# Scratch for the sums of x in a tile of its own, the keys turned behind the queries' scan, and one more tile of lag for the second layer

## The chip, the cores and the metric

The kernel runs on one core of one Trainium2 chip (trn2). The metric is the device time of one execution in microseconds (us); the median of three runs is given. A core has five engines that run their own queues in order and wait for one another by semaphores: TensorE (PE, with its weight loads PEld), VectorE (DVE), ScalarE (ACT), GpSimd (POOL) and SyncE (SP, which here only issues transfers). Transfers (DMA) run on 16 DMA engines.

## The reference

Two parts follow one another. The first is a gated linear attention over 4 batches, 8 heads, 768 positions and a head size of 48; the second a two-layer network with a squared relu, on 3072 tokens with a model size of 384 and a hidden size of 2048.

```python
f = 1 / (1 + exp(-f_logit))
for t in range(768):                       # per batch and head
    state = f[t][:, None] * state + outer(k[t], v[t])
    y[t] = q[t] @ state
x = y of all heads side by side            # 3072 x 384
h = maximum(x @ w_in, 0)
out = (h * h) @ w_out
```

## The kernel before

**Blocks, units, tiles.** The 768 positions are cut into 6 blocks of 128 positions (512 tokens with the 4 batches). The attention of a block is done in 4 units of two heads each; 16 of them (those of blocks 2 to 5, called 2_0 to 5_3 here) run inside the stream of the second part. The second part of a block has 16 tiles f of 128 hidden rows. A tile has a first layer (`up`, nine matmuls of 512 columns: three slices of the model size, each as three products of float16 halves), a squared relu with a split into halves gh and gl, and a second layer (`down`, nine matmuls: for each third e of the output the products of w's upper half with gl, w's lower half with gh, upper half with gh). The order of blocks is 1, second half of 0, 2, 3, 4, 5; tiles are counted through from the start of this order, so that block 2 has tiles 24 to 39 and blocks 3, 4, 5 have 40 to 55, 56 to 71, 72 to 87.

**The second layer lags.** In blocks 2 to 5 (`flow`) `owe` puts the three second-layer pieces of a finished tile into a queue, and `take` issues pieces from its front. In block 2, each tile takes three pieces and adds three; in a tile listed in `SKIP` it takes none, and the queue stays three longer from then on. gh and gl have `GBUF` = 5 buffers each.

**Pairs.** In blocks 3 to 5 the first layer of two tiles is done together (`pair`): eleven narrow steps of three matmuls with 256 columns, in place of six steps with 512. It needs sums of quarters of w (made earlier) and of x: t1 to t4 of `make_sums_x`. These are ten POOL subtractions and additions in float32 (line 586) into a scratch, which ACT (line 589) and DVE (line 590) then split into halves. They are issued at the last four tiles of the block before. The scratch lies in a hole of the tiles of w_out of f = 8 to 11: a w tile has 768 float32 columns as two halves of 384; the float16 weights take the first 192 float32 columns of each half, and `work` takes 128 columns behind them in either half. The results t1 to t4 go to holes of the tiles 0 to 7. A pair's relu, square and split run on ACT and POOL (`later`, lines 510 to 517) after the next pair's first two products.

**Units in the stream.** Each unit has a slot, a tile number of `SLOTS`: 12, 14, 19, 21 for block 2, 22, 27, 29, 33 for block 3, 35, 39, 43, 47 for block 4, 51, 55, 59, 63 for block 5. In the slot, TensorE computes the outputs of the unit before (stage Y), the added state and the scores of this one (D, lines 888, and S, line 907); D reads kn, the keys turned by 32x32 squares. The stages before it are hung on earlier tiles by `STAGE_AT` (blocks up to 2) and `STAGE_AT_LATER` (blocks 3 to 5): (tiles from the slot, place in the tile, stages). L loads f, k and q into fkq. G makes the gates (ACT, line 760), K scans the gates backwards for the keys' factors (line 767), k multiplies the keys (780), Q scans forwards for the queries' factors (789), q multiplies the queries (797). t (`squares`) turns the keys within squares on DVE (line 846) and writes them to DRAM in four transfers (`steps`, line 852); b (`back`) loads them in their new order as kn (line 859; one buffer). K, Q and t use the same row of fkq (`rr`) for their results. The fourth unit of a block has no keys of its own (its rows are gathered from the other three by stages m and l). SP issues transfers in the order of the program, and each waits for what it reads. Stage b stands three tiles before the slot; where the unit before has its slot in between, it stands in that unit's slot. Transfers x<-ys (lines 1026), which complete a block's x, are issued in the slot after the fourth unit's.

**The scratch called junk.** Line 205 (`sizes`, ACT) writes absolute values of weights that nobody reads, one pass per tile from tile 28 on, 32 in all; only their sum counts. It takes 384 of the 1560 float32 columns of a tile with one buffer.

Of the kernel before, what the change touches and what calls it, by code (L numbers as in the profile page):

```python
# [12 lines left out]
F32 = mybir.dt.float32  # L13
# [10 lines left out]
P = 128  # L24
B, H, S, D = 4, 8, 768, 48
DM, DFF = 384, 2048
# [5 lines left out]
NT = B * TB  # L32
NZ = B * NC
CZ = C + 1
ROWS = 64 + D
NJ = DM // P
# [36 lines left out]

STAGE_AT = ((-8, 1, "L"), (-6, 1, "GK"), (-5, 0, "v"), (-5, 1, "Q"), (-4, 1, "t"))
STAGE_AT_LATER = (
    (-8, 1, "L"), (-6, 1, "G"), (-5, 0, "vK"), (-5, 0.7, "k"), (-5, 1, "t"), (-3, 0, "Q"), (-3, 0.7, "q"),
)
LAST_AT = ((-5, 0, "v"),)

SLOTS = (12, 14, 19, 21, 22, 27, 29, 33, 35, 39, 43, 47, 51, 55, 59, 63, 67)  # L80
# [2 lines left out]
NQ = NT // 2  # L83
HB, HA = slice(0, NQ), slice(NQ, NT)
PAIRED = 3
SKIP = 6, 10
T_HOLES, T_WORK, S_WORK = (0, 4), 8, 12
S_FROM, S_STEPS = 10, 6

LATE = ((0, 2), (0.5, 2)), ((0.7, 2), (1, 2))  # L90
# [23 lines left out]
class Moe:  # L114
# [86 lines left out]
    def sizes(self, f, i):  # L201

        if not (f or i):
            self.junk = self.third_of("junk")[0][:, :DM]
        self.nc.scalar.activation(
            self.junk, self.w[f, i][:, 0], AF.Abs, scale=1.0 if i else 4.0,
            accum_out=self.sums[:, 2 * f + i : 2 * f + i + 1],
        )
# [324 lines left out]

    def work(self, f):

        return self.full[f, 1].bitcast(F32)[:, :, DM // 2 : DM // 2 + P]

    def make_sums_w(self, q):

        G = self.nc.gpsimd  # L540
        add, sub = ALU.add, ALU.subtract
        f, f2 = 2 * q, 2 * q + 1
        (a11, a12), (a21, a22) = (
            [[self.w[k, 0][:, i, j * P : (j + 1) * P] for i in range(2)] for j in range(2)] for k in (f, f2)
        )
        s, u = (self.work(S_WORK + 2 * (q % 2) + i)[:, 0] for i in range(2))
        out = self.sums_w(q)

        def split(n, t):
            G.tensor_copy(out=out[n][:, 0], in_=t)  # L550
            yield
            G.tensor_tensor(out=out[n][:, 1], in0=t, in1=out[n][:, 0], op=sub)
            yield

        def chain(t, *terms):
            for o, i0, i1, op in terms:
                G.tensor_tensor(out=o, in0=i0, in1=i1, op=op)  # L557
                yield

        yield from chain(s, (s, a21[0], a22[0], add), (s, s, a21[1], add), (s, s, a22[1], add))  # L560
        yield from split(0, s)
        yield from chain(u, (u, a11[0], a21[0], sub), (u, u, a11[1], add), (u, u, a21[1], sub))
        yield from split(2, u)
        yield from chain(s, (s, s, a11[0], sub), (s, s, a11[1], sub))
        yield from split(1, s)
        yield from chain(s, (s, a12[0], s, sub), (s, s, a12[1], add))
        yield from split(3, s)

    def make_sums_x(self, blk, x):

        nc, G = self.nc, self.nc.gpsimd
        add, sub = ALU.add, ALU.subtract
        wide = lambda t: t.rearrange("p (a n) -> p a n", a=2)
        (b11, b12), (b21, b22) = (
            [[wide(x[j][:, i, h]) for i in range(2)] for h in (HA, HB)] for j in range(2)
        )
        t1, t2, t3, t4 = (self.work(T_WORK + i) for i in range(4))
        out = self.sums_x(blk)
        for terms in (
            ((t1, b12[0], b11[0], sub), (t1, t1, b12[1], add), (t1, t1, b11[1], sub)),  # L580
            ((t3, b22[0], b12[0], sub), (t3, t3, b22[1], add), (t3, t3, b12[1], sub)),
            ((t2, t3, b11[0], add), (t2, t2, b11[1], add)),
            ((t4, b21[0], t2, sub), (t4, t4, b21[1], add)),
        ):
            for o, i0, i1, op in terms:
                G.tensor_tensor(out=o, in0=i0, in1=i1, op=op)  # L586
            yield
        for n, t in ((0, t1), (2, t3), (1, t2), (3, t4)):
            nc.scalar.copy(out=wide(out[n][:, 0]), in_=t)
            nc.vector.tensor_tensor(out=wide(out[n][:, 1]), in0=t, in1=wide(out[n][:, 0]), op=sub)  # L590
            yield

    def third_of(self, name):
# [72 lines left out]
def fast_path(ctx, tc, moe, ident, low, fkqT, vN, w, w4, out):  # L666
    nc = tc.nc
    V, G = nc.vector, nc.gpsimd
# [24 lines left out]
        out=mask0, in_=mask0, compare_op=ALU.is_ge, fill=0.0, base=0, pattern=[[1, TB]], channel_multiplier=-1,  # L693
    )
    G.memset(mask, 1.0)
    for r in (0, C):
        G.affine_select(
            out=mask[r : r + C], in_=mask[r : r + C], compare_op=ALU.is_ge, fill=0.0,
# [441 lines left out]
    with tc.manual_schedule(engines={ET.PE, ET.SP, ET.DVE, ET.Activation, ET.Pool}):  # L1140
# [6 lines left out]
        part = []  # L1147
# [5 lines left out]
        def hook(k, n, at, do):  # L1153
            while n >= len(order[k][1]):
                k, n = k + 1, n - len(order[k][1])
            hooks[k].setdefault((max(n, 0), at), []).append(do)
# [28 lines left out]
        back = 0  # L1185
        for un, last, at, soon, then in zip((*later, None), (None, *later), SLOTS, (*later[1:], None, None), (*SLOTS[1:], None)):
            if un:
                for n, place, stage in (STAGE_AT if un.early else STAGE_AT_LATER) if un.own else LAST_AT:
                    hook(0, at + n, place, lambda un=un, stage=stage: un.stage(stage))
                if un.own:  # L1190

                    if at - 3 > back:
                        hook(0, at - 3, 1, lambda un=un: un.stage("b"))
                    back = at

            def slot(un=un, last=last, soon=soon if soon and soon.own and then - 3 <= at else None):
                for who, stage in (last, "Y"), (un, "DS"), (last, "HX"), (un, "rMC"), (soon, "b"), (un, "ml" * bool(un and un.own)):
                    if who:
                        who.stage(stage)
                if last and not last.own:  # L1200
                    last.stage("hg")

            hook(0, at, 0.7, slot)
            if un:
                hook(0, at + 1, 0, lambda un=un: un.stage("s"))
# [34 lines left out]
        for blk in range(PAIRED, NBLK):  # L1240
            n = 2 * NF + LO + (blk - PAIRED) * NF - 4
            for at, place in ((0, 1), (1, 0.5), (1, 1), (2, 0.5), (2, 1), (3, 0), (3, 0.5), (3, 1)):
                hook(0, n + at, place, lambda blk=blk: advance_sums(blk, lambda: moe.make_sums_x(blk, xs[blk]), 1))
        for k, (blk, fs) in enumerate(order):
# [5 lines left out]
            if blk > 1:  # L1250
# [3 lines left out]
                if blk == NBLK - 1:  # L1254
                    obs = moe.third_of("ob_last")
                    items[-1:] = [(f,) for f in fs[-2:]]
                moe.flow(hooks[k], items, SKIP if blk == 2 else (), owed if blk == 2 else None)
            else:
# [157 lines left out]
@with_exitstack  # L1416
def tile_kernel(ctx: ExitStack, tc: tile.TileContext, fkqT, vN, w, w4, out):
    nc = tc.nc
    const = ctx.enter_context(tc.tile_pool(name="const", bufs=1))
    ident = const.tile([P, P], F32, name="ident")  # L1420
    low = const.tile([P, NBLK * NJ, B * NC], F32, name="low")
    sums = const.tile([P, (2 + NBLK) * NF + NBLK * NJ], F32, name="sums")
    moe = Moe(ctx, tc, const, sums, out)
    moe.hidden(ctx)
    with ExitStack() as fast:
        rv, obs = fast_path(fast, tc, moe, ident, low, fkqT, vN, w, w4, out)


    with tc.If(rv > 0):
        with ExitStack() as gen:  # L1430
            general_path(gen, tc, moe, ident, fkqT, vN, w, out)
        for e in range(NJ):
            nc.sync.dma_start(obs[e], out[NBLK - 1, e * P : (e + 1) * P])

    for e in range(NJ):
        for n, cs in tails(e):

            (nc.sync if n else nc.scalar).dma_start(out[NBLK - 1, e * P : (e + 1) * P, cs], obs[e][:, cs])
# [61 lines left out]
```

## Time and profile before

| | |
|---|---|
| median of 3 runs | 509.65 us (509.09 to 511.13) |
| profiled execution | 510.53 us, span 508.8 us |
| TensorE busy | 457.5 us (90%), mean granted clock 0.973 |
| ACT, DVE, POOL busy | 306.5, 280.0, 209.8 us |
| DMA | 47.90 MB, mean 94 GB/s |

The span runs from the first to the last instruction of the profiled execution. The granted clock is the share of TensorE's full clock (2.4 GHz) that it was given; the lower level is half of it. An engine's wait is the idle time ahead of an instruction, put down to what ended it.

### The profile page before, as it was taken

The page shows a single profiled execution, that of the slowest core. Times are in us where ns is not written, and L with a number is a line of the kernel's source. Part 1 is how long each engine was busy: PE and PEld are TensorE (multiplying, and loading weights), DVE is VectorE, ACT ScalarE, POOL GpSimd, SP SyncE. Part 2 cuts the span into 40 slices and gives each one's busy share as a digit, 9 for nine tenths or more (in the row PEclk, how much of TensorE's full clock was granted, in tenths as well). Part 3 has the DMA queues.
Part 4 walks back from the last instruction along what each step waited for, and adds up shares of the span by engine and source line. Part 5 has one row for each costly group of instructions (what it writes and reads, how often), then busy time and mean ns, then how long its engine had stood idle before and what let it go on. Part 6 is the DMA issues. An engine that isn't in the chain of part 4 may idle for free.

```text
span 508.8 us, 12206 instructions
## 1 busy us (share of the span) xinstructions
PE 457.5 (90%) x4903; PEld 262.0 (51%) x4906; DVE 280.0 (55%) x512; ACT 306.5 (60%) x709; POOL 209.8 (41%) x337
## 2 busy tenths in 40 slices
PE   8999899999998989998799899769999868999995
PEld 4655544444554535544266466436656534565652
DVE  8999826895646666656275455536524212324222
ACT  4679839855485546867358856537856532573650
POOL 5456436994865456440401321632131271313220
PEclk9999999999999999999799999889999987999998
DMA  8977075517354445143334041403200000100002
GB/s 301 279 279 236 14 252 196 205 36 160 82 147 114 99 122 135 22 130 54 96 71 138 20 119 25 125 10 63 79 1 2 12 6 0 63 0 1 1 0 70
DMA packets 65296, 47.90 MB, mean 94 GB/s; under 512 B 47440, under 2 KB 50768, under 8 KB 65232
## 3 DMA queue, kind: packets, MB, share of 16 engines
q1 hardware_dynamic: 64640, 46.19, 32.1%
q0 software_dynamic: 448, 0.73, 0.6%
q8 instruction: 40, 0.66, 0.5%
q14 instruction: 24, 0.20, 0.1%
q10 hardware_dynamic: 144, 0.13, 0.1%
HBM read 35.61 MB, written 7.86 MB: 85 GB/s over the span
## 4 chain that ended last, share of the span: by engine, by line
PE 37%; issue 16%; ACT 13%; POOL 11%; DVE 11%; DMA 8%; SPq 3%; POOLq 0%; DVEq 0%; ACTq 0%
PE po L365 16%; PE ph L309 10%; POOL gl L517 4%; PE cross L460 3%; POOL w L586 3%; ACT gh L514 3%; DMA raw<-in_w_dram 3%; DMA fkq<-in_fkqT_dram 3%; ACT st L510 2%; DMA steps<-fkq 2%; POOL w L192 2%; DVE gl L352 2%; PE line L460 2%; PE ds L907 1%; DVE fkq L789 1%
## 5 line engine op out<-in xcount | busy, mean ns | idle before, releaser
L365 PE MATMUL po<-gh,w 128*128 128x512 f16 x570 | 174.4, 388 | 18.3 <-POOL w L586 18.3
L365 PEld LDWEIGHTS <-w 128*128 128x128 f16 x864 | 84.0, 99 | 119.0 <-POOL w L586 20.4
L517 POOL TENSOR_TENSOR gl<-st,gh 128x512 f16<-128x512 f32 x46 | 54.0, 1195 | 173.4 <-ACT gh L514 173.4
L365 PE MATMUL po<-gl,w 128*128 128x512 f16 x288 | 111.2, 386 | 12.6 <-POOL gl L517 11.0
L309 PE MATMUL ph<-x,w 128*128 128x512 f16 x441 | 103.3, 380 | 3.2 <-DVE x L1019 2.5
L460 PEld LDWEIGHTS <-w 128*128 128x128 f16 x759 | 75.9, 100 | 35.2 <-issue 9.3
L505 ACT ACTIVATE st<-st 128x512 f32<-128x512 f32 x46 | 29.0, 631 | 86.5 <-DVE st L500 85.9
L309 PEld LDWEIGHTS <-w 128*128 128x128 f16 (+1 forms) x459 | 44.5, 98 | 57.4 <-issue 3.8
L352 DVE TENSOR_TENSOR gl<-ph,gh 128x512 f16<-128x512 f32 x48 | 32.8, 683 | 56.9 <-ACT gh L331 56.9
L327 ACT ACTIVATE ph<-ph 128x512 f32<-128x512 f32 x49 | 28.7, 586 | 54.1 <-PE ph L309 54.1
L500 DVE TENSOR_TENSOR st<-cross,st 128x512 f32<-128x512 f32 x23 | 15.9, 692 | 47.9 <-PE cross L460 47.9
L460 PE MATMUL cross<-x,w 128*128 128x256 f16 x276 | 38.4, 276 | 1.1 <-DVE ys L1019 0.9
L557 POOL TENSOR_TENSOR w<-w,w 128x128 f32<-128x128 f32 (+1 forms) x72 | 36.5, 507 | 4.3
L460 PE MATMUL cross<-w,w 128*128 128x256 f16 x207 | 35.3, 281 | 2.8 <-DVE st L489 1.6
L789 DVE TENSOR_TENSOR_SCAN fkq<-fz,dz 128x520 f32<-128x520 f32 x18 | 23.2, 1289 | 18.7 <-DMA steps<-fkq 18.3
L460 PE MATMUL line<-x,w 128*128 128x256 f16 x207 | 31.3, 280 | 0.0
L192 POOL TENSOR_TENSOR w<-wa,w 128x384 f16<-128x384 f32 x29 | 30.1, 1042 | 2.0
L187 POOL CAST w<-wa 128x384 f16<-128x384 f32 x29 | 19.9, 687 | 26.7 <-DVE wa L176 22.9
L767 DVE TENSOR_TENSOR_SCAN fkq<-fz,dr 128x520 f32<-128x520 f32 x18 | 23.3, 1295 | 12.2 <-ACT fz L760 12.2
L331 ACT ACTIVATE gh<-ph 128x512 f16<-128x512 f32 x48 | 28.7, 598 | 1.6
L328 ACT ACTIVATE ph<-ph 128x512 f32<-128x512 f32 x49 | 28.5, 582 | 1.5
L489 DVE COPY st<-cross 128x256 f32<-128x256 f32 x23 | 9.7, 420 | 35.7 <-PE cross L460 35.5
(184 smaller groups left out, 803.2 us busy)
## 6 DMA issues: line engine op xcount, KB each, us to landing
raw<-in_w_dram SPq DMA_DIRECT2D x33, 383.8 KB, 6.0
fkq<-in_fkqT_dram SPq DMA_DIRECT2D x15, 768.0 KB, 5.2
vn<-in_vN_dram SPq DMA_DIRECT2D x24, 192.0 KB, 4.9
steps<-fkq SPq DMA_DIRECT2D x48, 64.0 KB, 2.2
out_dram<-ob SPq DMA_DIRECT2D x12, 256.0 KB, 2.1
kn<-steps SPq DMA_DIRECT2D x13, 224.0 KB, 3.5
fkq<-in_fkqT_dram SPq DMA_DIRECT2D x9, 256.0 KB, 4.9
last_kq<-fkq SPq DMA_DIRECT2D x28, 64.5 KB, 3.1
```

The source lines that it names most:

```text
L192: (eng or nc.vector).tensor_tensor(out=w[:, 1], in0=a, in1=high, op=ALU.subtract)
L309: self.nc.tensor.matmul(self.ph[f], lhsT=w[:, i], rhs=x[:, j], start=first and n == 0, stop=last and n == 2)
L327: nc.scalar.activation(ph, ph, AF.Relu, scale=R_SCALE if self.half else 1.0)
L328: nc.scalar.activation(ph, ph, AF.Square)
L331: nc.scalar.activation(gh, ph, AF.Copy, accum_out=self.sums[:, n : n + 1])
L352: self.nc.vector.tensor_tensor(out=gl, in0=self.ph.pop(f), in1=gh if self.half else gh.bitcast(F32), op=ALU.subtract)
L365: self.nc.tensor.matmul(po[e], lhsT=l, rhs=r, start=f == fs[0] and i == 0, stop=f == fs[-1] and i == 2,)
L460: self.nc.tensor.matmul(out, lhsT=w[:, i], rhs=x[:, j], start=first and n == 0, stop=True, skip_group_check=True)
L505: nc.scalar.activation(st[:, r], st[:, r], AF.Relu, scale=R_SCALE)
L517: nc.gpsimd.tensor_tensor(out=wide(gl), in0=st[:, i::2], in1=wide(gh), op=ALU.subtract)
L557: G.tensor_tensor(out=o, in0=i0, in1=i1, op=op)
L789: V.tensor_tensor_scan(out=pp, data0=self.fz[:, : NZ * CZ], data1=dz, initial=0.0, op0=ALU.mult, op1=ALU.add)
```

## The change

1. The scratch for the sums of x moves from the holes of w tiles into the tile of which line 205 uses the first 384 columns: four contiguous pieces of 256 columns from column 512 on. The scratch for the sums of w stays where it was.
2. For units of blocks 3 to 5, Q moves from (-3, 0) to (-5, 1), q from (-3, 0.7) to (-3, 0), t from (-5, 1) to (-3, 0.7). Stage b moves from (-3, 1) to (-2, 0) (`BACK`); where the rule for "in between" holds for both places, b is issued in both.
3. `SKIP` gets tile 1 of block 2 besides 6 and 10, so that the second layer lags four tiles from block 2's tile 10 on, where it lagged three.

```diff
@@ -73,8 +73,9 @@
 
 STAGE_AT = ((-8, 1, "L"), (-6, 1, "GK"), (-5, 0, "v"), (-5, 1, "Q"), (-4, 1, "t"))
 STAGE_AT_LATER = (
-    (-8, 1, "L"), (-6, 1, "G"), (-5, 0, "vK"), (-5, 0.7, "k"), (-5, 1, "t"), (-3, 0, "Q"), (-3, 0.7, "q"),
+    (-8, 1, "L"), (-6, 1, "G"), (-5, 0, "vK"), (-5, 0.7, "k"), (-5, 1, "Q"), (-3, 0, "q"), (-3, 0.7, "t"),
 )
+BACK = -2, 0
 LAST_AT = ((-5, 0, "v"),)
 
 SLOTS = (12, 14, 19, 21, 22, 27, 29, 33, 35, 39, 43, 47, 51, 55, 59, 63, 67)
@@ -83,8 +84,8 @@
 NQ = NT // 2
 HB, HA = slice(0, NQ), slice(NQ, NT)
 PAIRED = 3
-SKIP = 6, 10
-T_HOLES, T_WORK, S_WORK = (0, 4), 8, 12
+SKIP = 1, 6, 10
+T_HOLES, S_WORK = (0, 4), 12
 S_FROM, S_STEPS = 10, 6
 
 LATE = ((0, 2), (0.5, 2)), ((0.7, 2), (1, 2))
@@ -201,7 +202,9 @@
     def sizes(self, f, i):
 
         if not (f or i):
-            self.junk = self.third_of("junk")[0][:, :DM]
+            junk = self.gp.tile([P, NJ * NZ * CZ], F32, tag="part", name="junk", bufs=1)
+            self.junk = junk[:, :DM]
+            self.work_x = [junk[:, NT + i * NQ : NT + (i + 1) * NQ] for i in range(4)]
         self.nc.scalar.activation(
             self.junk, self.w[f, i][:, 0], AF.Abs, scale=1.0 if i else 4.0,
             accum_out=self.sums[:, 2 * f + i : 2 * f + i + 1],
@@ -533,7 +536,7 @@
 
     def work(self, f):
 
-        return self.full[f, 1].bitcast(F32)[:, :, DM // 2 : DM // 2 + P]
+        return self.full[f, 1].bitcast(F32)[:, 0, DM // 2 : DM // 2 + P]
 
     def make_sums_w(self, q):
 
@@ -543,7 +546,7 @@
         (a11, a12), (a21, a22) = (
             [[self.w[k, 0][:, i, j * P : (j + 1) * P] for i in range(2)] for j in range(2)] for k in (f, f2)
         )
-        s, u = (self.work(S_WORK + 2 * (q % 2) + i)[:, 0] for i in range(2))
+        s, u = (self.work(S_WORK + 2 * (q % 2) + i) for i in range(2))
         out = self.sums_w(q)
 
         def split(n, t):
@@ -570,11 +573,10 @@
 
         nc, G = self.nc, self.nc.gpsimd
         add, sub = ALU.add, ALU.subtract
-        wide = lambda t: t.rearrange("p (a n) -> p a n", a=2)
         (b11, b12), (b21, b22) = (
-            [[wide(x[j][:, i, h]) for i in range(2)] for h in (HA, HB)] for j in range(2)
+            [[x[j][:, i, h] for i in range(2)] for h in (HA, HB)] for j in range(2)
         )
-        t1, t2, t3, t4 = (self.work(T_WORK + i) for i in range(4))
+        t1, t2, t3, t4 = self.work_x
         out = self.sums_x(blk)
         for terms in (
             ((t1, b12[0], b11[0], sub), (t1, t1, b12[1], add), (t1, t1, b11[1], sub)),
@@ -586,8 +588,8 @@
                 G.tensor_tensor(out=o, in0=i0, in1=i1, op=op)
             yield
         for n, t in ((0, t1), (2, t3), (1, t2), (3, t4)):
-            nc.scalar.copy(out=wide(out[n][:, 0]), in_=t)
-            nc.vector.tensor_tensor(out=wide(out[n][:, 1]), in0=t, in1=wide(out[n][:, 0]), op=sub)
+            nc.scalar.copy(out=out[n][:, 0], in_=t)
+            nc.vector.tensor_tensor(out=out[n][:, 1], in0=t, in1=out[n][:, 0], op=sub)
             yield
 
     def third_of(self, name):
@@ -1189,11 +1191,12 @@
                     hook(0, at + n, place, lambda un=un, stage=stage: un.stage(stage))
                 if un.own:
 
-                    if at - 3 > back:
-                        hook(0, at - 3, 1, lambda un=un: un.stage("b"))
+                    n, place = (-3, 1) if un.early else BACK
+                    if at + n > back:
+                        hook(0, at + n, place, lambda un=un: un.stage("b"))
                     back = at
 
-            def slot(un=un, last=last, soon=soon if soon and soon.own and then - 3 <= at else None):
+            def slot(un=un, last=last, soon=soon if soon and soon.own and then + (-3 if soon.early else BACK[0]) <= at else None):
                 for who, stage in (last, "Y"), (un, "DS"), (last, "HX"), (un, "rMC"), (soon, "b"), (un, "ml" * bool(un and un.own)):
                     if who:
                         who.stage(stage)
```

## Rows read from the trace of the kernel before

**Rows 1.** The page, busy time of each engine, share of the span, instructions
```profile
PE 457.5 (90%) x4903; PEld 262.0 (51%) x4906; DVE 280.0 (55%) x512; ACT 306.5 (60%) x709; POOL 209.8 (41%) x337
```

**Rows 2.** TensorE's waits: us in total, times, longest
```profile
PE po L365 <- POOL w L586: 18.3, 5, 5.4
PE po L365 <- POOL gl L517: 11.0, 19, 0.8
PE ph L309 <- DVE x L1019: 2.5, 1, 2.5
PE ph L971 <- DVE gl L352: 2.1, 3, 1.2
...
PE po L365 <- DVE part L642: 1.4, 1, 1.4
```

**Rows 3.** Timeline of TensorE, 237 to 252 us: start, us, line, tiles, [idle before]
```profile
237.56 2.11 PE L309 MATMUL ph<-x,w 128*128 128x512 f16 x9
239.51 0.38 PE L365 MATMUL po<-gl,w 128*128 128x512 f16 x1
245.33 1.03 PE L365 MATMUL po<-gh,w 128*128 128x512 f16 x2 [5.44 <-POOL w L586]
...
248.71 2.48 PE L309 MATMUL ph<-x,w 128*128 128x512 f16 x9
```

**Rows 4.** Windows behind the five stalls; PEclk is the third number from the end
```profile
245.30:252.00 6.70, 6.67 (x22) 2.68 (x23) 1.63 (x2) 1.88 (x5) 2.88 (x5) 0.69 0.16 47
328.30:334.00 5.70, 4.59 (x21) 2.64 (x21) 2.63 (x4) 4.39 (x11) 2.25 (x3) 0.73 0.23 70
337.40:343.00 5.60, 5.56 (x25) 2.94 (x26) 2.06 (x4) 0.00 (x0) 0.00 (x0) 0.70 0.07 12
413.10:419.00 5.90, 4.78 (x21) 2.73 (x21) 0.42 (x1) 3.48 (x8) 2.60 (x4) 0.71 0.00 0
421.40:428.00 6.60, 6.56 (x25) 3.19 (x26) 1.09 (x3) 0.00 (x0) 0.00 (x0) 0.58 0.00 0
```

**Rows 5.** Instructions of line 586: ns least/median/most, first and last start
```profile
L586 POOL TENSOR_TENSOR w<-w,x x21: 667/669/672, 241.7 to 420.7; 128x256 f32<-128x256 f32 x21
```

**Rows 6.** DVE's waits, as above
```profile
DVE fkq L789 <- DMA steps<-fkq: 18.3, 5, 5.1
```

**Rows 7.** Timeline of DVE, 142 to 158.5 us
```profile
146.50 1.13 DVE L846 STREAM_TRANSPOSE fkq<-fkq 128x512 f32<-128x512 f32 x1
...
153.40 1.25 DVE L789 TENSOR_TENSOR_SCAN fkq<-fz,dz 128x520 f32<-128x520 f32 x1 [5.08 <-DMA steps<-fkq]
154.57 0.66 DVE L352 TENSOR_TENSOR gl<-ph,gh 128x512 f16<-128x512 f32 x1
...
158.02 0.68 DVE L797 TENSOR_TENSOR fkq<-fkq 128x512 f32<-128x512 f32 x1
```

**Rows 8.** The page's groups: busy, mean ns of one | idle before
```profile
L331 ACT ACTIVATE gh<-ph 128x512 f16<-128x512 f32 x48 | 28.7, 598 | 1.6
```

**Rows 9.** Line 852, the transfers of steps, from issue to landing
```profile
DMA to landing us min/median/max: 2.1/2.2/3.8
```

**Rows 10.** Line 859, the load of kn, from issue to landing
```profile
DMA to landing us min/median/max: 3.2/3.5/5.1
```

**Rows 11.** Timeline of SP, 209 to 240 us (issues, waits between them included)
```profile
214.10 2.86 SPq L852 DMA_DIRECT2D steps<-fkq  x4
...
218.64 4.70 SPq L859 DMA_DIRECT2D kn<-steps  x2
```

**Rows 12.** Timeline of SP, 316 to 335 us
```profile
318.53 5.17 SPq L1026 DMA_DIRECT2D x<-ys  x6
323.80 0.61 SPq L750 DMA_DIRECT2D fkq<-in_fkqT_dram  x1
```

**Rows 13.** Timeline of ACT, 324 to 338 us
```profile
325.47 1.28 ACT L505 ACTIVATE st<-st 128x512 f32<-128x512 f32 x2 [2.49 <-DVE st L500]
329.02 0.63 ACT L760 ACTIVATE fz<-fkq 128x512 f32<-128x512 f32 x1 [2.27 <-DMA fkq<-in_fkqT_dram]
```

## The prediction

> **What bounds the kernel now.** I read the page first: TensorE is busy 457.5 of 508.8 us, every other engine at most 60% [rows 1]. So I asked what TensorE waits for. Two names hold two thirds of the waiting: POOL's line 586 with 18.3 us in 5 waits, and POOL's line 517 with 11.0 us in 19 [rows 2]. Below them stand waits on DVE (lines 1019, 352, 642), 6.0 us together.
>
> Line 586 makes the sums of x. The timeline of TensorE shows how it gets in the way [rows 3]. A step of the second layer issues three matmuls per e: upper half of w with gl, lower half of w with gh, upper half with gh. At 239.51 the first runs; the next stands for 5.44 us until POOL is done. The upper half is free, the lower is not. The scratch of before is two pieces of the same w tile (columns 192 to 319 of either half, in float32): from the first piece to the end of the second, that range covers the lower half of the weights. I conclude that TensorE waits for a range, not for data: it never reads those sums here. After the stall nine matmuls that took 2.11 us at 237.56 take 2.48 at 248.71: the granted clock has fallen to 1.2 GHz for a while. In the stretches behind the five stalls it is 0.58 to 0.73 on average [rows 4].
>
> Line 517 (gl of a pair) is the end of a chain, copy, square, gh, gl, that starts with the next pair; the second layer wants it 4 us later, and each pair loses up to 0.8 us [rows 2].
>
> On DVE the queries' scan of line 789 waits 18.3 us in 5 waits for the transfers of `steps` [rows 6]: the keys' turn and the scan use the same row of fkq, and the turn is written first. At 146.50 the turn, at 153.40 the scan, 5.08 us idle [rows 7]; behind it in the queue stood line 1019, for which TensorE then waited 2.5 us [rows 2].
>
> **The change part by part.** Terms are taken against the profiled run, 510.5 us (its span is 508.8).
>
> *Scratch of its own.* The 30 POOL instructions stay and keep 128x256 elements; all forms took 0.67 us [rows 5], and I cost the contiguous form the same. What goes is the overlap: 18.3 us [rows 2]. With the stalls goes the slow clock behind them: one minus the granted clock, times the stretch, is 2.1 + 1.5 + 1.7 + 1.7 + 2.8 = 9.8 us [rows 4]. Bounds for this: 5 (new stalls keep the clock low) to 9.8. Scratch is bufs=1 in a tile that ACT's line 205 writes in columns 0 to 383, the sums in 512 to 1535; rows 3 show that disjoint ranges don't wait.
>
> *SKIP at tile 1.* One more tile of second-layer work (three entries, nine matmuls) stays in the queue. A pair takes six entries; before, three old ones stood ahead of the new, now six, so a pair's gl is first read at the start of the pair after next, about 5 us later than now. The largest wait was 0.8, so all 11.0 us go. gh and gl have five buffers; four tiles in flight fit. At tile 1 itself TensorE skips the wait for line 642 (1.4 us). But two first-layer steps come back to back, and the tile after needs a bank that DVE frees behind three 0.7 us pieces of line 642 and the turn: I put 0.9 us there (0 to 2).
>
> *Queries before the turn.* The scan no longer waits. On TensorE that is worth 2.5 + 1.4 + 1.5 = 5.4 us (of the 2.1 us on line 352, 0.6 come from two back-to-back first-layer steps of the older skips, and stay) [rows 2]. Bounds: 0, if DVE is late again, to 6.
>
> What it costs: the turn, the four `steps` transfers and the load of kn now start 3 tiles before the slot in which TensorE reads kn (stage D); what queues behind a late kn is everything on TensorE. From the end of that tile's first layer: three ACT passes of 0.60 [rows 8], line 352 with 0.66, the turn 1.13 [rows 7], four issues of which the last comes some 2.0 after the first [rows 11], landing 2.2 (up to 3.8) after that [rows 9], kn 3.5 (3.2 to 5.1) [rows 10]. That is 11.3 us, 14.5 with the slowest landings. For the way TensorE needs three tiles of twice 1.95 us (nine matmuls, 237.56 to 239.51), 11.7 us [rows 3], and about 1 more, an estimate, for the outputs of the unit before: 12.7. In a plain unit kn is just in time. Not plain are: unit 3_0 (slot 22), whose turn stands behind slot 19's DVE pieces (155.2 to 158.0, 2.8 us) [rows 7], and which is now loaded twice: it is queued at tile 20 by the new rule and again in slot 21, and the second load of the one kn buffer waits for the first. How that looks is seen for unit 4_0, loaded twice already: two issues stretch over 4.70 us, and the second starts when the first has landed [rows 11]. So 11.3 + 2.8 + 3.5 = 17.6 against 14.7 (a slot lies between, some 2 us): 2.9 us. Unit 4_0 (slot 35): 14.8 against 12.7: 2.1. Unit 3_1 (slot 27), with one step of 1.95 skipped on the way: 0.3. The paired units have two thirds of a pair and a whole one, 18 wide matmuls and 33 half as wide a pair, 0.217 us for a wide one, 12.4 us, and the outputs: 0. I add 0.7 for transfers in each other's way: 6 us, between 0 and 14 (slowest landings at the five unpaired units).
>
> A page of the Trainium skill speaks against this part: DMA: Bandwidth & Descriptors, Rules for kernel authors, says to issue a transfer early and wait for it late, so that its fixed cost is covered. The change issues one later. No row shows the loads uncovered yet; by that rule the second rival below would be the forecast.
>
> *What stands behind the stalls.* With line 586 out of the way, ACT comes next in block 3's last pairs: its gates of 329.02 waited 2.27 us for a load of fkq [rows 13], issued at 323.80 behind six transfers that last 5.17 us [rows 12]. Nothing in the change moves those. Today TensorE stands still there anyway. Then it will begin the pair near 326, while ACT is in the passes of 325.47 [rows 13], do 12 narrow and three wide matmuls (1.95 us), and wait from about 327.9 for ACT's copy of its first products, which can end at 330.8 (329.65, then line 205 and the copy, 0.6 each): 3.0 us (0 to 4.5, with the clock). Block 2's like wait goes, since the turn's transfers no longer stand in SP's queue before it.
>
> Sum: 510.5 - 18.3 - 9.8 - 11.0 - 5.4 + 6.0 + 3.0 + 0.9 = 475.9. The median of the runs, 509.65, is 0.9 below the profiled run, and a fall of the clock behind a new stall would cost about as much: 476 us. All the gains without new waits give 466; the bounds together 460 to 495.
>
> **Rivals.**
> 1. *The turned keys come late everywhere.* For: plain units have only 1.4 us to spare, and one load took 5.1. Against: medians. If each of the nine units loses 3 us, 27 instead of 6: 497 us. The clock may fall with it.
> 2. *The same, and slower than before.* From where does this decide? All else given, slower than 512 needs 42 us in nine units, 4.7 each, so a chain of 17 us in a plain unit. Its slowest rows give 14.5; SP's queue (x<-ys, loads of fkq) would have to add 3 in each. Then 512 to 520.
> 3. *The scratch is still tied.* If order is kept for the whole new tile, ACT's line 205, one per tile while blocks 3 and 4 get their sums, takes turns with POOL's ten instructions (7 us), and ACT passes the wait to TensorE. Two of three blocks get their stalls back, 5.4 + 2.7 + 4.5 and 5.3 of clock: 494 us. Against it: rows 3.
> 4. *Even less comes back.* All transfers in time: 460 to 466.
>
> **How the numbers follow.** Forecast (466 to 487): 0.71. Rival 1 (487 to 507): 0.13; rival 2: 0.04; rival 3: 0.07; rival 4: 0.05. The range from 465 to 492 leaves out rival 2, most of rivals 1 and 4 and half of 3, about 2 in 10. A difference under 0.5% (2.5 us) can't be told from none with this kernel. Faster takes all cases but rival 2 and a tail of rival 1 at no change: 0.93, same 0.03, slower 0.04.
>
> **What the next profile would show.** Line 586 among TensorE's releasers: gone; line 517 too, or under 1 us. PEclk at full speed at the ends of blocks 2, 3 and 4. No wait of line 789 for `steps`. New: matmuls of line 888 (stage D) waiting for the load of kn, at slots 22 and 35 above all, and 14 loads of kn instead of 13; one wait of line 460 on ACT's line 481 at the end of block 3. Wrong it would be if line 888 waits at every unit, if ACT's line 205 waits for POOL's line 586, or if the clock falls behind the new waits.

## The result and the profile after

The changed kernel takes 467.86 us (median of 4 runs, 466.19 to 469.73), the kernel before 510.39 us on the same chip (509.09 to 511.57; four runs, of which the table before has three). The ratio is 0.9168, with a 95% interval from 0.9124 to 0.9212: 42.5 us or 8.3% faster. The profiled execution took 468.25 us, its span 466.5 us. 476 us had been forecast, with a range from 465 to 492: the sign and the range held, and the forecast was 8 us too high. In `after` the line numbers are two or three higher than before: line 365 is now 368, 517 is 520, 586 is 588, 888 is 890, 859 is 861, 760 is 762, 481 is 484.

The page of the kernel after, as [rows 1]:

```profile
PE 446.0 (96%) x4906; PEld 260.2 (56%) x4906; DVE 279.4 (60%) x512; ACT 306.0 (66%) x709; POOL 211.6 (45%) x337
```

The span fell by 42.3 us. Of this 30.8 us are idle time of TensorE (508.8 - 457.5 = 51.3 before, 466.5 - 446.0 = 20.5 after), and 11.5 us are busy time, at the same number of weight loads (4906 in both pages).

TensorE's waits after (us in total, times, longest), as [rows 2]:

```profile
PE cross L463 <- ACT st L484: 4.7, 6, 3.1
PE ds L890 <- issue: 2.4, 2, 1.3
PE ds L890 <- DMA kn<-steps: 1.4, 1, 1.4
```

The two names that led [rows 2], the sums of x and gl on POOL, are gone from the list; so is the wait of 2.5 us for DVE's x. New are one wait on ACT of 3.1 us and waits of line 890 (stage D): 1.4 us for kn at slot 22, and 1.1 us at slot 35, which the list puts under "issue", idle time that nothing in the profile is seen to end (the other 1.3 us of that line stood in the kernel before as well).

A stretch of the timeline of TensorE after that answers to [rows 3]:

```profile
236.64 0.38 PE L368 MATMUL po<-gl,w 128*128 128x512 f16 x1
236.86 0.59 PE L368 MATMUL po<-gh,w 128*128 128x512 f16 x2
237.29 0.38 PE L368 MATMUL po<-gl,w 128*128 128x512 f16 x1
```

Of POOL in the same stretch:

```profile
236.73 0.67 POOL L588 TENSOR_TENSOR junk<-x,x 128x256 f32<-128x256 f16 x1
237.48 3.82 POOL L588 TENSOR_TENSOR junk<-junk,x 128x256 f32<-128x256 f32 x4
```

While POOL makes the sums of x, TensorE issues a step of three matmuls in 0.65 us (236.64 to 237.29) and stops for nothing. The windows over the work that stood behind the five stalls of [rows 4], found by counting matmuls from the start (the granted clock is the third number from the end):

```profile
238.60:245.30 6.70, 6.70 (x82) 3.33 (x84) 4.98 (x8) 4.90 (x15) 4.08 (x6) 1.00 0.50 115
314.40:320.00 5.60, 5.54 (x24) 2.84 (x24) 3.54 (x7) 3.41 (x10) 3.72 (x5) 0.70 0.48 111
319.00:324.60 5.60, 5.29 (x151) 4.14 (x150) 4.61 (x8) 2.46 (x6) 1.78 (x2) 1.00 0.02 3
384.20:390.10 5.90, 5.90 (x41) 3.87 (x40) 2.46 (x5) 4.35 (x10) 5.59 (x8) 1.00 0.00 0
387.80:394.40 6.60, 6.60 (x48) 4.55 (x47) 4.48 (x8) 3.88 (x10) 4.08 (x5) 1.00 0.00 0
```

TensorE has its full clock in four of the five. In the second, which now lies behind the wait on ACT, it has 0.70 on average over 5.6 us, which costs 1.7 us.

The new wait on ACT is the forecast one [rows 12, 13]. The timeline of SP after:

```profile
302.66 5.22 SPq L1028 DMA_DIRECT2D x<-ys  x6
307.98 0.60 SPq L752 DMA_DIRECT2D fkq<-in_fkqT_dram  x1
```

Of ACT:

```profile
312.81 0.63 ACT L762 ACTIVATE fz<-fkq 128x512 f32<-128x512 f32 x1 [2.71 <-DMA fkq<-in_fkqT_dram]
...
313.85 0.56 ACT L484 COPY st<-cross 128x512 f32<-128x512 f32 x1
```

Of TensorE, there and at slot 22:

```profile
166.83 0.31 PE L983 MATMUL py<-rx,sx 48*48 48x64 f32 x2 [0.76 <-ACT sx L826]
...
169.65 0.52 PE L890 MATMUL ds<-vn,kn 64*64 64x48 f32 x25 [1.42 <-DMA kn<-steps]
...
310.72 0.59 PE L368 MATMUL po<-gh,w 128*128 128x512 f16 x2
314.46 0.49 PE L463 MATMUL cross<-w,w 128*128 128x256 f16 x3 [3.15 <-ACT st L484]
```

The load of fkq goes out behind six transfers of x, ACT's gates stand 2.71 us for it, the copy of line 484 stands behind them, and TensorE stands 3.15 us for the copy.

### The profile page after: what moved, and what is told of

It reads as the page before. It is cut to its first block, busy times and chain, and to the rows that moved or that the text cites. A ratio compares the mean times of both kernels' runs of the same rounds, so it can differ in the third digit from the quotient of the medians.

```text
span 466.5 us, 12214 instructions
## 1 busy us (share of the span) xinstructions
PE 446.0 (96%) x4906; PEld 260.2 (56%) x4906; DVE 279.4 (60%) x512; ACT 306.0 (66%) x709; POOL 211.6 (45%) x337
## 4 chain that ended last, share of the span: by engine, by line
PE 65%; DMA 10%; DVE 9%; ACT 7%; POOL 4%; issue 3%; SPq 2%; POOLq 0%; ACTq 0%; DVEq 0%
PE po L368 30%; PE ph L312 13%; PE cross L463 10%; PE line L463 5%; DMA fkq<-in_fkqT_dram 4%; DMA raw<-in_w_dram 3%; POOL w L193 2%; PE ds L909 2%; PE ds L890 2%; DMA kn<-steps 2%; POOL w L188 1%; DVE fkq L791 1%; DVE gl L355 1%; PE py L973 1%; SPq L1028 1%
## 5 line engine op out<-in xcount | busy, mean ns | idle before, releaser
L368 PE MATMUL po<-gh,w 128*128 128x512 f16 x570 | 170.5, 381 | 0.0
L368 PEld LDWEIGHTS <-w 128*128 128x128 f16 x864 | 83.7, 98 | 80.7 <-issue 1.3
L368 PE MATMUL po<-gl,w 128*128 128x512 f16 x288 | 109.9, 382 | 0.0
L463 PEld LDWEIGHTS <-w 128*128 128x128 f16 x759 | 74.3, 98 | 35.0 <-issue 9.2
L463 PE MATMUL cross<-w,w 128*128 128x256 f16 x207 | 34.2, 274 | 4.7 <-ACT st L484 4.7
L463 PE MATMUL line<-x,w 128*128 128x256 f16 x207 | 30.1, 273 | 0.0
L517 ACT ACTIVATE gh<-st 128x512 f16<-128x512 f32 x46 | 28.6, 622 | 0.7
```

What stands on the lines that cost most here:

```text
L368: self.nc.tensor.matmul(po[e], lhsT=l, rhs=r, start=f == fs[0] and i == 0, stop=f == fs[-1] and i == 2,)
L463: self.nc.tensor.matmul(out, lhsT=w[:, i], rhs=x[:, j], start=first and n == 0, stop=True, skip_group_check=True)
L517: nc.scalar.activation(wide(gh), st[:, i::2], AF.Copy, accum_out=self.sums[:, n : n + 1])
```

## The experiments

Ratios are to the kernel before, from runs on the same chip in each case; the medians of before lay between 510.4 and 512.5 us. So 0.01 of a ratio is 5.1 us, and a difference of two ratios below 0.005 is not told apart from none.

**The parts alone.** First the scratch without the rest (the tile for line 205's scratch also gives `work_x`, and the sums of x use it):

```diff
-        t1, t2, t3, t4 = (self.work(T_WORK + i) for i in range(4))
+        t1, t2, t3, t4 = self.work_x
```

> The kernel before with the scratch in its own tile alone (lag and order as before). My theory: TensorE waited for a range of the w tiles; its five waits for line 586 go (18.3 us, and 0.16 us each for a pipeline that has to refill), with them the slow clock behind (9.8), and in block 3's last pairs about 3 us come back as a wait for ACT's copy behind a late load of fkq, perhaps 2 more at the end of block 2, where the load is later than in the changed kernel: 484 to 491 us, 11 us of waits for line 517 as before. Rival, order kept for the whole scratch tile: ACT's line 205 waits for POOL's line 586, and only block 5's share of the gain is seen: 498 us or more.

Measured: 489.52 us, ratio 0.9562 (0.9528 to 0.9596). TensorE's waits in this kernel (line 519 is gl on POOL):

```profile
PE po L367 <- POOL gl L519: 11.5, 20, 0.8
PE cross L462 <- ACT st L483: 3.5, 5, 2.3
```

The sums of x no longer hold TensorE; line 205 doesn't take them up (rival 3 falls); the wait on ACT appears at once.

**Is it the range?** The scratch stays in the w tiles in two pieces, but each of POOL's instructions is issued as two, one for each piece, so that no access spans the weights between them:

```diff
-                G.tensor_tensor(out=o, in0=i0, in1=i1, op=op)
+                for r in range(2):
+                    G.tensor_tensor(out=o[:, r], in0=i0[:, r], in1=i1[:, r], op=op)
```

> The kernel before, scratch where it was, but each of the ten POOL instructions done as two, one for each half of the w tile, so that no single access runs over the lower half of the weights; the data, the places and the order stay. If TensorE waited for the range of one access, the five waits go although the scratch still lies in the w tiles: 484 to 492 us, with POOL some 2 us longer per block (20 pieces of 0.43 for 10 of 0.67). If order is kept for the whole tile, or for the data, nothing moves: 508 to 513.

Measured: 489.66 us, ratio 0.9552 (0.9517 to 0.9586), the same as with a scratch of its own. TensorE's waits:

```profile
PE po L365 <- POOL gl L517: 11.7, 20, 0.8
PE cross L460 <- ACT st L481: 3.4, 5, 2.2
```

And POOL's instructions of the sums, median 426 ns each:

```profile
L587 POOL TENSOR_TENSOR w<-w,x x42: 420/426/1360, 242.1 to 406.4; 128x128 f32<-128x128 f32 x42
```

Twice 426 ns is more work than 669 [rows 5], in the same tiles and columns, and yet the stalls are gone. So the stalls came from the range that one access with two pieces covers, not from the tile, the columns or POOL's speed.

**The lag alone.**

```diff
-SKIP = 6, 10
+SKIP = 1, 6, 10
```

> The kernel before with tile 1 in SKIP alone. My theory: all 19 waits for line 517 go, 11.0 us and 0.16 each of refill, the 1.4 us wait for line 642 too, and the five stalls at line 586 stay (one may be a tile later and shorter): 494 to 498 us. By the profile after, the end also gets shorter by about 2 us, since the last pieces of the first third now lie further ahead of the end: then 492 to 496. Rival: the next wait of the pair chain takes over, 503 or more.

Measured: 486.07 us, ratio 0.9503 (0.9461 to 0.9545), better than either theory. TensorE's waits:

```profile
PE po L365 <- POOL w L586: 8.7, 5, 3.6
PE ph L971 <- DVE gl L352: 5.1, 3, 3.3
```

Line 517 is gone, as expected. The four runs lie between 480.69 and 488.39 us, the widest spread of these kernels, and the profiled one is the fastest of them (mean granted clock 0.995, in the others 0.986 to 0.988), so its waits stand for less than the median. What I had not seen: line 586's waits fell as well, from 18.3 to 8.7 us in 5 waits, by 4.5, 1.9, 0.9, 1.4 and 1.0 us in their order. Three entries more stand ahead of the one that meets POOL's range, and nine matmuls take 1.95 us [rows 3]; that fits the average of 1.9 us, not the single waits, so how the lag shortens each of them is not shown. What is shown is that the lag also does half of the scratch's work, so that the gains of the two parts overlap. And a new wait of 3.3 us stands on line 352 (at 192.32), of which more below.

**The order alone.** Q, q, t and b at the new places, the rest as before:

```diff
-    (-5, 1, "t"), (-3, 0, "Q"), (-3, 0.7, "q"),
+    (-5, 1, "Q"), (-3, 0, "q"), (-3, 0.7, "t"),
```

> The kernel before with the order of the units of blocks 3 to 5 alone (queries first, turn later, load of kn in the new place). My theory: the scan's waits go, worth 5.4 us and some refills to TensorE, and 4 us come back as late loads of kn at slots 22 and 35: 506 to 511 us, no clear change. Rival 1, late keys at each unit: 520 and more. Rival 2, the early scan is worth more than its waits because SP's queue is freed before block 2's end: 500 to 505.

Measured: 502.77 us, ratio 0.9823 (0.9781 to 0.9865): the rival's figure. TensorE's waits:

```profile
PE po L366 <- POOL w L587: 15.5, 6, 4.7
...
PE ds L889 <- DMA kn<-steps: 2.6, 1, 2.6
```

The scan's waits are gone, and slot 22 waits for kn. That the sum is better than the first theory comes in part from the end of block 2, where the stall on the sums of x is 1.88 us instead of 5.44 [rows 3]: the transfers of x go out at 233.49 here, in before at 236.91. SP before:

```profile
231.30 2.62 SPq L852 DMA_DIRECT2D steps<-fkq  x4
...
236.91 3.82 SPq L1026 DMA_DIRECT2D x<-ys  x6
```

SP in the kernel with the order alone, where the turn's transfers don't stand there:

```profile
233.49 4.48 SPq L1027 DMA_DIRECT2D x<-ys  x6
```

**The order taken out of the whole.** The changed kernel with the old `STAGE_AT_LATER` and the old place of b:

> The changed kernel with the old order of queries and turn (scratch of its own and the skip at tile 1 stay). Theory: with the two larger parts in, the order is still worth something, since the scan's waits for the steps transfers (5.4 us on TensorE) come back and ACT's gates at the end of block 2 wait for the load of fkq (about 1.6 us, as in the kernel with the scratch alone), while the two late loads of kn (4.3 us) go: 469 to 473 us. Rival: the skip hides DVE's lateness, so the scan's waits cost nothing here, and only the late loads are left to tell: 463 to 466 us.

Measured: 477.57 us, ratio 0.9318 (0.9296 to 0.9339). It is 0.0150 above the change, 7.7 us, where 469 to 473 us had been expected: the direction held, the size didn't. TensorE's waits:

```profile
PE ph L972 <- DVE gl L354: 5.2, 3, 3.4
PE cross L462 <- ACT st L483: 4.3, 6, 2.7
PE ph L311 <- DVE x L1020: 2.5, 1, 2.5
PE cross L972 <- DVE gl L354: 2.0, 1, 2.0
PE cross L462 <- DVE st L491: 1.9, 4, 0.7
```

DVE at the time of the longest of these:

```profile
191.62 1.27 DVE L790 TENSOR_TENSOR_SCAN fkq<-fz,dz 128x520 f32<-128x520 f32 x1 [3.76 <-DMA steps<-fkq]
192.81 0.66 DVE L354 TENSOR_TENSOR gl<-ph,gh 128x512 f16<-128x512 f32 x1
```

At 193.52 TensorE has waited 3.37 us for this gl, the same place as the 3.3 us in the kernel with the lag alone. In the kernel before, the scan waits as long in all [rows 6], but the three waits on line 352 that TensorE has of it are 2.1 us together [rows 2].

**Which part makes the scan dear?** Two kernels with two parts each: scratch and order, lag and order.

> Scratch of its own and the new order, no skip at tile 1. Theory: what makes the scan's waits dear in the full kernel (the order is worth 7.7 us there) is the skip, which lets TensorE arrive at the pieces that DVE is late with; without the skip the order brings the 5.4 us of before and the 1.6 us at block 2's end and costs the 4.3 us of the late kn, so 2 to 5 us against the kernel with the scratch alone: a ratio to before of 0.946 to 0.953 (484 to 488 us). Rival: the order is worth 8 us whatever stands beside it: 0.938 to 0.942 (480 to 482 us).

Measured: 484.58 us, ratio 0.9485 (0.9451 to 0.9519), 3.9 us better than the scratch alone.

> The skip at tile 1 and the new order, scratch left in the w tiles. Theory: with the skip the order is worth as much as in the full kernel, 7 to 10 us against the kernel with the skip alone, and no wait of some 3 us on line 352's piece near 192 us is left: a ratio to before of 0.931 to 0.937 (476 to 480 us). Rival: the order is worth 2 to 5 us here, since the stalls on line 586 take up its gain: 0.940 to 0.947 (481 to 485 us).

Measured: 477.17 us, ratio 0.9322 (0.9292 to 0.9353), 9.3 us better than the lag alone. TensorE's waits there:

```profile
PE po L366 <- POOL w L587: 7.9, 4, 3.2
...
PE ds L889 <- DMA kn<-steps: 2.1, 1, 2.1
```

The 3.3 us are gone, and the stalls on the sums are much what they were with the lag alone (7.9 for 8.7). So this wait needs the lag and the old order together: 3.3 and 3.4 us in the two kernels with both, 0.3 us at the same place in the kernels with the old order and no lag (193.60 in the kernel before), none with the new order. As I read it, the tile that takes no second-layer pieces brings TensorE 1.95 us sooner to its next need of DVE, and the wait of 1.4 us for line 642 that it skips makes it 3.35; the wait grew by 3.0. All eight cases together, as ratios:

| scratch | lag | order | ratio | | scratch | lag | order | ratio |
|---|---|---|---|---|---|---|---|---|
| - | - | - | 1 | | yes | yes | - | 0.9318 |
| yes | - | - | 0.9562 | | yes | - | yes | 0.9485 |
| - | yes | - | 0.9503 | | - | yes | yes | 0.9322 |
| - | - | yes | 0.9823 | | yes | yes | yes | 0.9168 |

The scratch is worth 0.044 alone (22 us) and 0.015 (8 us) once lag and order are in; the lag 0.050 alone, 0.032 as the last; the order 0.018 alone, 0.008 beside the scratch, 0.018 beside the lag, 0.015 as the last. So the order is worth more with the lag only where the scratch is in; without the scratch the order also shortens the stalls on the sums (15.5 for 18.3 us alone).

**Which of the new waits come from what?** In the change, unit 3_0's and 4_0's stage b is queued twice. Now only once:

```diff
+                        queued.add(un.n)
...
-                for who, stage in (last, "Y"), (un, "DS"), (last, "HX"), (un, "rMC"), (soon, "b"), (un, "ml" * bool(un and un.own)):
+                for who, stage in (last, "Y"), (un, "DS"), (last, "HX"), (un, "rMC"), (soon, "b" * bool(soon and soon.n not in queued)), (un, "ml" * bool(un and un.own)):
```

> The changed kernel, but a unit whose turn and load of kn were already queued ahead is not given them a second time in the slot before its own. Theory: the second load, which stands behind the first in the one kn buffer, is why TensorE waits at slots 22 and 35 (3.1 and 1.2 us); without it 463.5 to 466 us, and no matmul waits for kn behind the prologue. Rival: the place of the turn alone makes kn late, so slot 22 still waits 2 us or more: 466.5 to 468.5 us.

Measured: 462.49 us, ratio 0.904 (0.9012 to 0.9068), 6.6 us better than the change (0.9168 - 0.904 = 0.0128). SP ahead of slot 22, first in the change:

```profile
162.04 4.91 SPq L861 DMA_DIRECT2D kn<-steps  x2
```

then in this kernel:

```profile
162.24 0.56 SPq L861 DMA_DIRECT2D kn<-steps  x1
```

The four transfers of `steps` ahead of it start at 156.31 in both. Slot 22's D begins at 166.54 instead of 169.65 (3.1 us), slot 35's at 223.51 instead of 227.76 (1.1 us more); behind the prologue one matmul still waits for kn, 0.18 us at 189.00 (slot 27). Of the 3.1 us, 1.42 are the wait for kn, which ended last, and 0.76 a wait for ACT's line 826 ahead of it. SP in the change, at the second of the two loads:

```profile
166.44 0.52 SPq L861 DMA_DIRECT2D kn<-steps  x1
```

It goes out when the first has landed, and that is before 166.54, where D begins when b is issued once. The place of the turn alone is therefore early enough here; the second load was late. Two more us come at the end of block 3: the wait on ACT is 2.57 us instead of 3.15, and the clock doesn't fall behind it (a mean clock of 1.000 over the profiled run). That this was to be had by the edit itself I can't say; the profile shows it for one execution, and of the other four one has a mean of 1.000 too, the rest 0.996 to 0.999.

The load of fkq that ACT waits for, half a tile earlier, ahead of the six transfers of x:

```diff
+                    if stage == "L" and at > 39:
+                        place = 0.5
```

> The changed kernel, with the loads of fkq of the units behind slot 39 queued half a tile earlier, ahead of the slot's six transfers of x. Theory: the wait of ACT's gates for that load at the end of block 3 (2.7 us), TensorE's wait for ACT behind it (3.15 us), and the slow clock behind that (about 1.7 us) go: 462.5 to 465.5 us. Rival 1: the load then holds up the transfers of x and with them the sums, the same time is lost on line 588 instead: 467 to 469 us. Rival 2: ACT is late there for its own work, whatever the load does: 466 to 468 us.

Measured: 465.41 us, ratio 0.9073 (0.9051 to 0.9094), 4.9 us better than the change and at the edge of what was expected. TensorE's waits:

```profile
PE cross L463 <- ACT st L484: 1.9, 6, 0.4
PE cross L973 <- DVE st L503: 1.6, 1, 1.6
```

The wait of 3.1 us is gone, so the load's place was its cause, not ACT's own work. About half comes back some 8 us later as a wait on DVE (1.6 us). The profiled execution doesn't show the whole gain: in it the clock fell behind slot 22, which none of this edit's work touches.

Both together:

> Both of these edits together. Theory: they act at different places, so the gains add: 459 to 462.5 us. Rival: one gain is taken up by the other's wait, as it was between the parts of the change: 462.5 to 466 us.

Measured: 460.67 us, ratio 0.8997 (0.8978 to 0.9016): 1.9% under the change, and faster than any other version here. The two gains don't quite add (6.6 + 4.9 = 11.5, together 8.8). The difference of 2.7 us is little more than the noise; that the clock at the end of block 3 is counted in both would account for part of it, which is not shown. The page:

```profile
PE 443.7 (97%) x4903; PEld 259.5 (57%) x4906; DVE 281.5 (61%) x512; ACT 306.0 (67%) x709; POOL 214.9 (47%) x337
```

## Why the prediction was right, and where it was not

**Right in mechanism.** TensorE waited for a range (shown by splitting the access), gl's wait went with the lag (shown by the lag alone), the scan's waits with the order. The three new waits came where they were put: slot 22 first, then slot 35, no other unit; ACT's gates at the end of block 3, one wait, 3.15 us for 3.0; a short one for a bank near tile 26. Rivals 1 and 3 fall: D waits at two slots, and line 205 never waits for POOL. So does rival 2, which needed late keys in every unit. One of the prediction's signs of being wrong did come: the clock fell behind the new wait on ACT. It cost 1.7 us, where the forecast had allowed 0.9.

**Sizes, idle time.** Forecast: 34.7 us of waits less (18.3 + 11.0 + 5.4), 9.9 us more (6.0 + 3.0 + 0.9), 24.8 us less in all. Measured: 30.8 us less. The 6.0 us between the two are most of the 8 us by which the forecast was too high. The terms:
- *Late kn, 6.0.* Beside the kernel that issues b once, slot 22 lost 3.1 us (forecast 2.9), slot 35 1.1 (forecast 2.1), slot 27 and the others nothing (forecast 0.3 and 0.7; for slot 27 the prediction's own figures, 11.3 against 12.7 less 1.95, give 0.55). That is 4.2 us, of which 3.3 are idle time of TensorE: the working for slot 22 held, and the additions for the rest were too careful. Both loads were late by being issued twice, not by their place, as that kernel shows. The Trainium skill's rule (DMA: Bandwidth & Descriptors, Rules for kernel authors) is to issue early and wait late. The trace bears it out for the second loads alone; that the turn and the first load start later shows as a wait for kn of 0.18 us at slot 27 and no other.
- *Bank wait, 0.9.* 0.3 us at 188.72.
- *Left out.* The pairs' waits on DVE's line 489 (1.6 us in 4 waits before, 1.6 to 1.9 in every kernel with the old order, none in those with the new), and the end of the kernel: from TensorE's last step of line 368 to the end of the span 5.8 us instead of 7.8. The last transfers of the output are issued there. In the five kernels that have both the lag and the order this end takes 5.3 to 6.7 us, in the seven others 7.2 to 8.4, so it goes with these two together; by what way is not shown.
- *Line 642, 1.4.* The forecast counted it with the order's 5.4. With the order alone 1.0 us of it stays; it is the lag that takes it away.

**Sizes, busy time.** The forecast took 9.8 us for the slow clock behind the stalls. Four of the windows over that work now stand at 1.00, and the one behind the new wait costs 1.7: 8.1 us less. Another 3.4 us of busy time went, which the forecast didn't have. The timeline of the change shows what it most likely is. The last two matmuls ahead of the wait on ACT start at 310.72 and show 0.59 us, so they end at 311.31, and 3.15 us of idle time follow. Where nothing waits, the next matmul starts 0.43 us behind such a pair (236.86 to 237.29), not 0.59. So each wait loses some 0.16 us beyond its idle time. The change leaves 22 idle stretches over 0.1 us of 51 before: 29 times 0.16 is 4.6 us, an estimate, beside the 3.4. The other kernels bear it out: over all twelve, TensorE's busy time less what the slow clock added runs from 442.7 us (23 such stretches, b issued once) to 448.8 (46, the split access), and a straight line through them rises by 0.15 us a stretch, with single kernels up to 1.6 us off it. So besides the idle terms above, the price of a removed wait was mis-sized in the sum: I took it as its idle time.

**Right in sum, not in shares.** The forecast gave the order next to nothing (5.4 gained, 6.0 lost) and the scratch 28.1 us, less 3.0 for the wait on ACT behind it. Measured as the last part added, the order brought 7.7 us and the scratch 8. The terms of the prediction were read from one trace in which TensorE was late everywhere; each part then changes what the others are worth. One by one the three parts bring 0.111 of the time before, together 0.083. The forecast's terms may be added up for all parts at once, as they were here, but no one of them is that part's worth.

## What to carry to other kernels

Before a scratch is put into the gaps of a live tile in several pieces, ask which range one access covers: splitting the instruction or making the pieces contiguous took away the same 22 us. When a stage is moved, look for places where it is now queued twice: a second load into a single buffer turned a just-in-time transfer into a late one at two slots and cost about 1%. And take the worth of an edit from the profile that it will run in: each wait removed lets TensorE meet the next late engine sooner, as the lag did with DVE, so edits that look unrelated should be tried together.

## What the runs showed of the hardware

The granted clock (full is 1.00, the lower level half of it) doesn't follow from the length of one wait. At the same place, behind 3.31 us of idle time in the kernel with the lag alone, the clock stays at its full level:

```profile
192.30:198.00 5.70, 5.68 (x143) 3.63 (x144) 5.25 (x11) 2.90 (x8) 5.02 (x12) 1.00 0.41 81
```

and behind 3.37 us in the kernel without the order it doesn't:

```profile
193.50:197.00 3.50, 3.48 (x128) 2.84 (x129) 3.47 (x7) 2.18 (x6) 3.06 (x8) 0.67 0.02 5
```

Behind 2.57 us it stayed at 1.00 in the kernel that issues b once:

```profile
309.60:312.00 2.40, 2.32 (x14) 1.36 (x14) 1.84 (x5) 2.37 (x7) 0.58 (x1) 1.00 0.41 119
```

In the kernel with lag and order, behind a wait of the same 2.57 us, it fell:

```profile
397.00:400.00 3.00, 2.59 (x14) 1.60 (x15) 0.00 (x0) 0.00 (x0) 0.36 (x1) 0.79 0.00 0
```

At that same place in the program, behind 2.57 us once more, it stayed full in the kernel with the lag alone:

```profile
399.20:402.00 2.80, 2.71 (x20) 1.97 (x21) 0.44 (x1) 0.00 (x0) 0.03 (x1) 1.00 0.00 0
```

So a forecast can give a price for the clock behind a wait of this size (1.7 us in the change), but from the wait's length alone not whether it will be paid. What else decides wasn't tried.
